# Gate logits in spare columns of the P·V bank, an earlier key load and one more GpSimd copy, in an attention + mixture-of-experts kernel

## The chip, the cores and the metric

The kernel runs on one core of one Trainium2 chip, as one launch. The metric is the device time of the launch in microseconds, median of the runs made: 671.96 us for the kernel before (three runs, 670.69 to 673.42 us).

## The reference

Attention over B = 4 batches, 8 heads, 768 positions of 64 features, then a mixture of 8 experts, two of them for each of the 3072 tokens:

```python
# attention, S=768, block=32, window=16, nb=24
k_sum = k.reshape(B, H, nb, block, D).max(axis=3)
v_sum = v.reshape(B, H, nb, block, D).mean(axis=3)
scores_l = where(|pos_i - pos_j| < 16, scale * q @ k.T, -1e9)
scores_s = scale * q @ k_sum.T + log(block)
a = softmax(concat([scores_l, scores_s], -1))
x = a @ concat([v, v_sum])                 # 3072 tokens x 512
# experts: w1 (8, 512, 1024), w2 (8, 1024, 512)
noisy = x @ w_gate + log1p(exp(x @ w_noise)) * noise
top2 = two largest of 8, weights = softmax of the two
out[token] = sum over its two experts e: weight * relu(x @ w1[e]) @ w2[e]
```

Each query sees its local window and one "block sum" for every block of 32 keys: the maximum of the block's keys (key maxima) and the mean of its values (block sums of V).

## The kernel before

**Stages.** Up to 138 us the attention and the gate run, then the expert products (lines 842 and 893) until 664 us, then the last stores. The attention is a loop `for t in range(-2, 23)` over 24 tiles of 128 tokens (6 tiles a batch), software-pipelined: an iteration t works on five tiles at once. In the order of issue an iteration does

- `load_q(t+5)` on SyncE's queue;
- `norm(t-1)`: VectorE reads the finished P·V tile `o` and writes `x` (lines 361, 365, 367);
- `scores(t+2)` on TensorE (316), `smax(t+2)` on VectorE (323, a row maximum `nm`), `p_trans(t+1)` on TensorE (339) into the two PSUM buffers named `pt`, which ScalarE copies out as `pts` (342); `mask_sums(t+3)` (306); `sexp(t+2)` on ScalarE (331); `kx_local(t+3)`, GpSimd copies of local keys;
- `av_space(t)`: the PSUM tile `o` (one buffer of two banks of 512 columns); `x_pe(t-1)` (376) into `pt` and ScalarE's copy `xt` of it; `av(t)` (352), the P·V product of tile t into `o`;
- `v_load(t+3)` and `x_out(t-2)` (the tile's `x` to DRAM as `xd`, line 371) on SyncE's queue.

Beside these stand the pieces of a table: `at(time, f, ...)` puts f into the iteration at a fractional time, and `run(t + 0.1)` and the like call what is due. An iteration issues the times t+0.02, t+0.1, t+0.3, t+0.31 and t+0.4 ahead of `av(t)`, and t+0.8 and t+0.9 behind it. The instructions of an engine run in the order of issue.

**The gate.** Tokens are gated in batches of four tiles. For batch b, with its four `xt` there, `gate_gt` (394) makes 32 logit rows of each tile on TensorE in a `pt` buffer, `gate_gc` copies them out as `lt` (VectorE, 402), `gate_gl` transposes that (408) into another `pt` buffer an iteration later, and `gate_gd` copies the result out as `lg` (415). For batches 0 to 3 these stand in iterations 5, 9, 13, 17 (`gate_gt`, `gate_gc`) and 6, 10, 14, 18 (`gate_gl`, `gate_gd`); for batch 4 both fall into iterations 21 and 22. Then `gate_a` (ScalarE), `gate_b` (VectorE, 439 to 451: the two largest of eight), `gate_m`, and `gate_c` (TensorE, 475 to 479) count and place the tokens; `gate_v` (528 to 578) builds lists.

**P·V's banks.** `o` is `[128, 2, 512]` in f32. `av` uses 4 x 65 = 260 columns of each bank (`GO` = 260). Behind them, the gate's small products (475 to 479) use columns 260 to 339 of the first bank.

**Keys and block sums.** Keys of batch b+1 come in two loads of three tiles, `load_k`, at the times `KL`; `k_piece` takes their block maxima on VectorE (230) at the times `KP`; `kx_sum` puts these into the score operand. `v_sums` makes the block sums of V on TensorE (256), copies them out, and makes some of the copies for the other tiles on GpSimd (272, 273); `v_rest` spreads the rest by DMAs from SBUF to SBUF (278, 281). All DMAs of the attention are issued by SyncE, in order, over eight semaphores: each waits for the landing of the one that is eight places earlier.

**Weights.** `w_load` brings weights (727, tile `stg`), ScalarE rounds them (`w_part`, 747 to 749), VectorE makes the remainders.

Of the kernel before, what the change touches and what calls it, by code (L numbers as in the profile page):

```python
# [8 lines left out]
F32 = mybir.dt.float32  # L9
# [11 lines left out]
P = 128  # L21
TS = S // P
NT = B * TS
# [40 lines left out]
def attn_moe(ctx, tc, qt, kt, vt, wgn, noise, w1, w2, out):  # L64
# [184 lines left out]
    def v_sums(b):  # L249
        if b:  # L250
            pt = psum.tile([P, HP, P], F32, name="pt", bufs=2).rearrange("p a b -> p (a b)")
        else:
            pt = psum.tile([P, 2, 512], F32, name="o")[:, 0]
        for j in range(TS):
            for g in range(4):
                nc.tensor.matmul(pt[32 * g:32 * g + NB, 0:C4], ind[:, j, :], VE[b % 2][:, j, C4 * g:C4 * g + C4],
                                 start=(j == 0), stop=(j == TS - 1), skip_group_check=True)
        x, y = VE[b % 2][W:W + NB], [z[0:NB] for z in VD[b % 2]]
        for g in range(4):
            i, o = pt[32 * g:32 * g + NB, 0:C4], slice(C4 * g, C4 * g + C4)  # L260
            if b == 3 and g % 2:
                nc.scalar.activation(x[:, 0, o], i, AF.Copy)
            elif b:
                nc.vector.tensor_copy(x[:, 0, o], i)
            else:
                nc.vector.tensor_copy(x[:, 0, o], i)
        if b == 1:
            nc.gpsimd.tensor_copy(y[0], x[:, 0])
        if b == 0:
            for i in range(3):  # L270
                if i:
                    nc.gpsimd.tensor_copy(x[:, i], x[:, 0])
                nc.gpsimd.tensor_copy(y[i], x[:, 0])

    def v_rest(b):
        x = VE[b % 2][W:W + NB]
        j = 1 if b else 3
        nc.sync.dma_start(x[:, j:], x[:, 0, None, :].to_broadcast([NB, TS - j, VB]))
        if b:
            for y in VD[b % 2][b == 1:]:  # L280
                nc.sync.dma_start(y[0:NB], x[:, 0])  # L281
# [104 lines left out]

    LT = {}

    def gate_gt(b):
        t0, t1 = BATCH[b]  # L390
        pt = psum.tile([P, HP, P], F32, name="pt", bufs=2)[:, 0]
        for c in range(DC):
            for i in range(GN):
                nc.tensor.matmul(pt[32 * i:32 * i + 32], wg32[:, c, :], XT[t0 + i][:, c, :],
                                 start=(c == 0), stop=(c == DC - 1), skip_group_check=True)
        LT[b] = pt
# [6 lines left out]
        else:  # L403
            nc.scalar.activation(LT[b], pt, AF.Copy)

    def gate_gl(b):
        pt = psum.tile([P, HP, P], F32, name="pt", bufs=2)[:, 0]
        nc.tensor.transpose(pt, LT[b], ident)
        LT[b] = pt

    def gate_gd(b):
        LG[b] = work.tile([P, GN, 16], F32, name="lg")
        x = LT[b].rearrange("p (t e) -> p t e", e=32)[:, :, 0:16]
        if b < 5:
            nc.vector.tensor_copy(LG[b], x)
        else:
            nc.scalar.activation(LG[b], x, AF.Copy)
# [507 lines left out]
    def at(t, f, *a):  # L925
        todo.setdefault(round(t, 3), []).append((f, a))
# [36 lines left out]
            at(W0[i] + 3 + k + 0.9, w_part, i, k, 0)  # L963
            at(W0[i] + 4 + k + 0.1, w_part, i, k, 1)
    VS = [5, 8, 15]
    KP = [-3, -3, -2, -1, 1, 2]
    KP0 = [1, 1, 1, 2, 2, 2]
    KL = [-6, -6, -6, -3, -3, -3]
    VL = [(0, 0, 0, 1, 1, 1), (4, 4, 5, 5, 6, 6), (10, 10, 11, 11, 12, 13)]
    for b in range(B - 1):  # L970
        for j in range(TS):
# [8 lines left out]
    for i in range(3):  # L980
        at(4.9 + 2 * i, fill, i)
    at(20.8, last_init)
    for t, i, k in ((19.9, 4, 0), (20.9, 4, 1), (21.9, 5, 0), (22.9, 5, 1), (22.9, 6, 0)):
        at(t, w_part, i, k, 0)
    for k in range(2):
        at(22.3, w_part, 4, k, 1)
# [4 lines left out]
    at(22.8, gate_p, 4)  # L991
    for b in (0, 1, 3, 2):
        u = BATCH[b][1] + 2
        at(u - 0.7, gate_gt, b)
        at(u - 0.6, gate_gc, b)
        at(u + 0.3, gate_gl, b)
        at(u + 0.4, gate_gd, b)
        at(u + 0.9, gate_a, b)
        at(u + 1.1, gate_b, b)
        at(u + 1.9, gate_m, b)  # L1000
        at(u + 2.9, gate_p, b)
        at(u + 2.3, lambda b, t: gate_c(b, PO[t]), b, u + 2)
        at(u + 3.02, lambda b, t: gate_d(b, PO[t]), b, u + 2)
        at(u + 3.9, gate_e, b)
        if b == 3:
            continue
        at(u + 4.1, gate_v, b)
        if b == 2:
            at(u + 4.2, gate_o0, b)
            at(u + 5.31, lambda b, t: gate_t0(b, PO[t]), b, u + 5)  # L1010
            at(u + 6.02, lambda t: gate_u0(PO[t]), u + 5)
            break
        z = u + 6
        at(z + 0.1, gate_o, b)
        at(z + 0.9, gate_f, b, (0,))
        at(z + 1.9, gate_f, b, (1,))
        at(z + 2.31, lambda b, t: gate_t(b, PO[t]), b, z + 2)
        at(z + 3.02, lambda b, t: gate_u(b, PO[t]), b, z + 2)
    at(20.1, decode, TB0[:, :, 0], TB0.bitcast(F32)[:, :, 1], 0, 3)
    at(21.3, gate_gt, 4)  # L1020
    at(21.4, gate_gc, 4)
    at(21.9, gate_gl, 4)
    at(22.02, gate_gd, 4)
    at(22.03, gate_a, 4)

    def run(t):
        for f, a in todo.pop(round(t, 3), []):
            f(*a)
# [5 lines left out]
    for t in range(-2, NT - 1):  # L1034
        if QBUF <= t + QA < NT:
            load_q(t + QA)
        u = t + 3
        if t >= 1:
            norm(t - 1, (lambda: kx_sum(u)) if u < NT else None)
        run(t + 0.02)  # L1040
        run(t + 0.03)
        if t + 2 < NT:
            scores(t + 2)
        if t == -1:
            q_piece(2)
            q_piece(3)
        run(t + 0.5)
        if t + 2 < NT:
            smax(t + 2)
        if 0 <= t + 1 < NT:  # L1050
            p_trans(t + 1, 0)
            p_trans(t + 1, 1)
        if t + 3 < NT:
            mask_sums(t + 3)
        if t + 2 < NT:
            sexp(t + 2, (0, 1) if t + 3 < NT else (0,))
        if u < NT and t >= 1:
            kx_local(u)
        run(t + 0.1)
        run(t + 0.2)  # L1060
        if t >= 0:
            av_space(t)
        run(t + 0.3)
        run(t + 0.31)
        if t >= 1:
            x_pe(t - 1)
        run(t + 0.4)
        if t >= 1:
            x_copy(t - 1)
        if t + 3 == NT:  # L1070
            sexp(t + 2, (1,))
        if t >= 0:
            av(t)
        run(t)
        run(t + 0.8)
        run(t + 0.9)
        if 0 <= t and t + 3 < NT:
            v_load(t + 3)
        if t >= 2:
            x_out(t - 2)  # L1080
# [7 lines left out]
    av(NT - 1)  # L1088
    gate_c(4, og)
    x_tr(0, 2, xp[:, 1].rearrange("p (a b) -> p a b", a=DC), False)  # L1090
    w_part(6, 1, 0)
    x_halves(0, 2, 0)
    x_pe(NT - 2)
    x_copy(NT - 2)
    norm(NT - 1)
    x_halves(0, 2, 1)
    w_part(7, 0, 0)
    w_part(7, 1, 0)
    gate_d(4, og)
    gate_e(4)  # L1100
    attn.close()
# [25 lines left out]
    for t in range(NT - 3, NT - 1):  # L1127
        x_out(t)
    low = {}
    for i in range(2):  # L1130
        bank()

    def first(f, mid=None):
        low[f] = mm1(0, 0, f, mid, False)
# [3 lines left out]
        x_copy(NT - 1)  # L1138

    def last_logits():  # L1140
        gate_gl(5)
        gate_gd(5)
        gate_a(5)

# [1 line left out]
    for x in HT:  # L1146
        nc.gpsimd.memset(x[:, :, CAPS[0]:], 0.0)
    x_out(NT - 1)
    gate_gt(5)
    gate_gc(5)  # L1150
    gate_v(3)
    low[0]()
# [3 lines left out]
    gate_p(5)  # L1156
    gate_o0(3)
    first(2)
    low[1]()
    gate_v(4)  # L1160
    first(3, lambda: gate_c(5, og))
# [198 lines left out]
```

## Time and profile before

| | before |
|---|---|
| median of three runs | 671.96 us (670.69 to 673.42) |
| profiled execution, its time | 675.12 us |
| its span, first to last instruction | 673.3 us |
| TensorE busy | 650.2 us (97%) |
| VectorE / ScalarE / GpSimd busy | 340.6 / 252.1 / 217.1 us |
| mean granted TensorE clock | 0.993 |

"Busy" is the time in which an engine has an instruction under way. Rows of the timeline begin with the start of a group of instructions and its duration, both in us; the brackets at the end of a row tell how long the engine idled before it and what it waited for. PE is TensorE, DVE VectorE, ACT ScalarE, POOL GpSimd, SP SyncE; `o<-hth,pts` reads "writes o, reads hth and pts". `hth`, `htl`, `ve`, `vd` are buffers that hold V in the attention. PEclk is the TensorE clock that the throttle granted, 1.00 being full speed.

### The profile page before, as it was taken

What the parts mean: (1) busy time and instruction counts of PE and PEld (TensorE: products, weight loads), DVE (VectorE), ACT (ScalarE), POOL (GpSimd) and SP (SyncE); (2) the same over time, 40 slices, a digit from 0 to 9 for tenths busy, and PEclk for the clock granted to TensorE, in tenths of its full rate; (3) what the DMA queues carried; (4) which work ended last, traced back from release to release, by engine and by line L of the source; (5) the groups of instructions that cost most, each with busy time, mean ns of one, the idle gap of its engine ahead of it and who ended that gap; (6) DMA issues with size and microseconds to landing.
All of it is one profiled execution on the core that took longest, in us unless ns stands there. A gap on an engine that the chain in (4) does not pass through costs nothing.

```text
span 673.3 us, 13939 instructions
## 1 busy us (share of the span) xinstructions
PE 650.2 (97%) x5485; PEld 379.9 (56%) x5485; DVE 340.6 (51%) x747; ACT 252.1 (37%) x570; POOL 217.1 (32%) x408
## 2 busy tenths in 40 slices
PE   8899799899999999999999999999999999999994
PEld 7678687655545544554455446544664455446541
DVE  5758799789794651265125513551264145312210
ACT  4867788841252450154015401530253045102100
POOL 4442134203265314431443144314431332321041
PEclk9999899999999999999999999999999999999998
DMA  9999999665297776267626753684378339521021
GB/s 299 309 276 297 307 311 320 226 219 140 108 258 210 213 177 211 85 172 174 211 84 173 186 190 96 177 203 152 95 197 229 121 86 234 148 76 48 1 92 48
DMA packets 93883, 120.50 MB, mean 179 GB/s; under 512 B 53577, under 2 KB 56913, under 8 KB 93808
## 3 DMA queue, kind: packets, MB, share of 16 engines
q1 hardware_dynamic: 82128, 83.24, 43.6%
q0 software_dynamic: 11680, 36.27, 16.9%
q8 instruction: 45, 0.74, 0.5%
q14 instruction: 30, 0.25, 0.1%
HBM read 82.03 MB, written 25.82 MB: 160 GB/s over the span
## 4 chain that ended last, share of the span: by engine, by line
PE 82%; DMA 9%; DVE 4%; SPq 2%; ACT 1%; issue 0%; POOL 0%; POOLq 0%; DVEq 0%; ACTq 0%
PE h L842 38%; PE pt L893 35%; DMA kb<-in_kt_dram 3%; PE h L893 2%; PE pt L890 2%; DMA xd<-x 2%; DMA htl<-in_vt_dram 2%; DMA ve<-ve 1%; PE pt L339 1%; DMA ve<-in_vt_dram 1%; DVE nm L323 1%; PE s L316 1%; PE o L352 1%; SPq L281 1%; DMA q<-in_qt_dram 1%; ACT p L331 1%
## 5 line engine op out<-in xcount | busy, mean ns | idle before, releaser
L842 PE MATMUL h<-xte,w1h 128*128 128x384 f16 (+4 forms) x1024 | 195.0, 331 | 1.1 <-DVE xte L818 1.1
L848 ACT ACTIVATE hth<-h 128x384 f16<-128x384 f32 (+4 forms) x128 | 63.7, 498 | 264.8 <-PE h L842 253.4
L842 PEld LDWEIGHTS <-w1h 128*128 128x128 f16 x1024 | 99.6, 98 | 73.0 <-issue 2.5
L89 POOL DMA_INDIRECT out_dram<-y,tb x48 | 52.9, 1101 | 234.4 <-DVE y L903 218.0
L893 PEld LDWEIGHTS <-hth 128*128 128x128 f16 x768 | 75.1, 98 | 89.3
L851 DVE SCALAR_TENSOR_TENSOR htl<-h,hth 128x384 f16<-128x384 f32 (+4 forms) x128 | 72.6, 568 | 70.0 <-ACT hth L848 63.7
L842 PE MATMUL h<-xte,w1l 128*128 128x384 f16 (+4 forms) x512 | 106.9, 331 | 0.0
L903 DVE SCALAR_TENSOR_TENSOR y<-pt,tb,prev 128x512 f32<-128x512 f32 x42 | 31.5, 751 | 144.9 <-PE pt L893 144.8
L89 POOL DMA_INDIRECT xg<-xd,tb x53 | 55.1, 1040 | 117.7 <-DVE x L806 68.9
L893 PE MATMUL pt<-w2l,hth 128*128 128x512 f16 x360 | 85.0, 379 | 0.0
L893 PE MATMUL pt<-w2h,hth 128*128 128x512 f16 x360 | 85.0, 379 | 0.0
L893 PE MATMUL pt<-w2h,htl 128*128 128x512 f16 x360 | 85.0, 379 | 0.0
L842 PEld LDWEIGHTS <-w1l 128*128 128x128 f16 x512 | 50.0, 98 | 35.5
L893 PEld LDWEIGHTS <-htl 128*128 128x128 f16 x384 | 37.6, 98 | 45.3
L754 DVE SCALAR_TENSOR_TENSOR w2l<-stg,w2h 128x1024 f16<-128x1024 f32 x28 | 34.3, 1225 | 38.4 <-ACT w2h L736 38.4
L331 ACT ACTIVATE p<-s,nm 128x120 f32<-128x120 f32 x192 | 51.1, 376 | 0.8
L736 ACT ACTIVATE w2h<-stg 128x1024 f16<-128x1024 f32 x28 | 29.5, 1054 | 54.2 <-DMA stg<-in_w_dram 54.2
L89 POOL DMA_INDIRECT prev<-out_dram,tb x42 | 43.8, 1043 | 13.2 <-issue 13.2
L754 DVE SCALAR_TENSOR_TENSOR w1l<-stg,w1h 128x1024 f16<-128x1024 f32 x28 | 34.3, 1224 | 21.1 <-ACT w1h L736 20.7
L736 ACT ACTIVATE w1h<-stg 128x1024 f16<-128x1024 f32 x28 | 29.4, 1050 | 11.4 <-DMA stg<-in_w_dram 11.4
L805 ACT ACTIVATE x<-xg 128x512 f16<-128x512 f32 (+4 forms) x48 | 29.8, 622 | 8.7 <-DVE y L901 3.7
L806 DVE TENSOR_TENSOR x<-xg,x 128x512 f16<-128x512 f32 (+4 forms) x48 | 32.7, 682 | 0.0
(225 smaller groups left out, 649.5 us busy)
## 6 DMA issues: line engine op xcount, KB each, us to landing
stg<-in_w_dram SPq DMA_DIRECT2D x64, 512.0 KB
q<-in_qt_dram SPq DMA_DIRECT2D x24, 256.0 KB
xd<-x SPq DMA_DIRECT2D x24, 256.0 KB
out_dram<-xg SPq DMA_DIRECT2D x8, 768.0 KB
kb<-in_kt_dram SPq DMA_DIRECT2D x6, 768.0 KB
hth<-in_vt_dram SPq DMA_DIRECT2D x12, 260.0 KB
htl<-in_vt_dram SPq DMA_DIRECT2D x16, 195.0 KB
ve<-in_vt_dram SPq DMA_DIRECT2D x12, 260.0 KB
```

What stands on the lines that cost most here:

```text
L89: return nc.gpsimd.indirect_dma_start(**kw)
L331: nc.scalar.activation(PE_[t][:, a, hp, :], SC[t][:, a, hp, :], AF.Exp, bias=NM[t][:, 1, a, hp:hp + 1], scale=0.125)
L736: nc.scalar.activation(WT[e][n + "h"][:, i % 4, :], SG[e, i], AF.Copy, scale=sc)
L754: nc.vector.scalar_tensor_tensor(lo, SG[e, i], sc, hi, op0=OP.mult, op1=OP.subtract)
L805: nc.scalar.activation(xs[:, :DM], x, AF.Copy)
L806: nc.vector.tensor_tensor(xs[:, DM:], x, xs[:, :DM], op=OP.subtract)
L842: nc.tensor.matmul(ph[:, :n], w[wn][:, c, f * P:(f + 1) * P], x[:, xo + c, c0:c1], start=(k == 0), stop=(k == 11))
L848: nc.scalar.activation(hh[:, f, c0:c1], ph[:, :n], AF.Relu)
L851: nc.vector.scalar_tensor_tensor(hl[:, f, c0:c1], ph[:, :n], 0.0, hh[:, f, c0:c1], op0=OP.max, op1=OP.subtract)
L890: nc.tensor.matmul(py[64 * i:64 * i + 64, :HD], hx[:, f, c * P:c * P + 64], wv[:, f, HD * i:HD * i + HD], start=st, stop=sp, skip_group_ch ...
L893: nc.tensor.matmul(py, hx[:, f, c * P:c * P + P], wv[:, f, :], start=st, stop=sp)
L903: nc.vector.scalar_tensor_tensor(y, py[:, :d], gw, pv[:, :d], op0=OP.mult, op1=OP.add)
```

## The change

Four things change.

1. `gate_gt` and `gate_gl` no longer take a `pt` buffer. They write 128 columns (340 to 467) of the first bank of the P·V tile that the iteration at hand uses: `PO[t]`, `PO[21]` for batch 4, and `og` for batch 5. For batch 4 the copy `lg` is made by ScalarE in place of VectorE.
2. The second key load of a batch is issued at -3.1 in place of -3, that is at the end of the iteration before, ahead of `v_load` and `x_out`.
3. The fourth key maximum of a batch is taken one iteration later (`KP`), those of the first prefetched batch one iteration later in four of six (`KP0`); `kx_sum(6)` is moved behind them.
4. `v_sums(0)` makes one more 24x520 copy on GpSimd, and the DMA of `v_rest(0)` carries two tiles in place of three. Some roundings of weights on ScalarE (`w_part`) stand later, and two empty takes of a PSUM bank ahead of the first expert are gone.

```diff
         if b == 0:
-            for i in range(3):
+            for i in range(4):
                 if i:
                     nc.gpsimd.tensor_copy(x[:, i], x[:, 0])
-                nc.gpsimd.tensor_copy(y[i], x[:, 0])
+                if i < 3:
+                    nc.gpsimd.tensor_copy(y[i], x[:, 0])
 
     def v_rest(b):
         x = VE[b % 2][W:W + NB]
-        j = 1 if b else 3
+        j = 1 if b else 4
...
-    def gate_gt(b):
+    GC = GO + 80
+
+    def gate_gt(b, o):
         t0, t1 = BATCH[b]
-        pt = psum.tile([P, HP, P], F32, name="pt", bufs=2)[:, 0]
+        pt = o[:, 0, GC:GC + P]
...
-    def gate_gl(b):
-        pt = psum.tile([P, HP, P], F32, name="pt", bufs=2)[:, 0]
+    def gate_gl(b, o):
+        pt = o[:, 0, GC:GC + P]
...
     def gate_gd(b):
-        if b < 5:
+        if b < 4:
             nc.vector.tensor_copy(LG[b], x)
...
-    KP = [-3, -3, -2, -1, 1, 2]
-    KP0 = [1, 1, 1, 2, 2, 2]
-    KL = [-6, -6, -6, -3, -3, -3]
+    KP = [-3, -3, -2, 0, 1, 2]
+    KP0 = [1, 1, 2, 2, 3, 3]
+    KL = [-6, -6, -6, -3.1, -3.1, -3.1]
...
-    for t, i, k in ((19.9, 4, 0), (20.9, 4, 1), (21.9, 5, 0), (22.9, 5, 1), (22.9, 6, 0)):
+    for t, i, k in ((19.9, 4, 0), (20.9, 4, 1), (22.9, 5, 0), (22.9, 5, 1)):
...
-        at(u - 0.7, gate_gt, b)
+        at(u - 0.69, lambda b, t: gate_gt(b, PO[t]), b, u - 1)
...
-        at(u + 0.3, gate_gl, b)
+        at(u + 0.3, lambda b, t: gate_gl(b, PO[t]), b, u)
...
-    at(21.3, gate_gt, 4)
+    at(21.31, lambda: gate_gt(4, PO[21]))
-    at(21.9, gate_gl, 4)
+    at(21.9, lambda: gate_gl(4, PO[21]))
...
-            norm(t - 1, (lambda: kx_sum(u)) if u < NT else None)
+            norm(t - 1, (lambda: kx_sum(u)) if u < NT and u != TS else None)
...
+        if u == TS:
+            kx_sum(u)
...
-    w_part(6, 1, 0)
+    w_part(6, 0, 0)
...
-    w_part(7, 0, 0)
-    w_part(7, 1, 0)
+    w_part(6, 1, 0)
...
-    for i in range(2):
-        bank()
...
-        gate_gl(5)
+        gate_gl(5, og)
...
-    gate_gt(5)
+    gate_gt(5, og)
...
+    for k in range(2):
+        w_part(7, k, 0)
```

What becomes of the order, at three places. Line numbers of the kernel after stand one to four higher.

TensorE in iteration 10, from the transpose of the gate's logits to the P·V product of tile 10. Before:

```order
L408 MATMUL pt<-ident,lt 128x128 [waits Activation_49]
L376 MATMUL pt<-ident,x 128x128 [waits DVE_49,Activation_49]
L376 MATMUL pt<-ident,x 128x128 x3
L352 MATMUL o<-ve,pts 64x65
L352 MATMUL o<-vd_100,pts 64x65 [waits DMAHW5_49]
```

After:

```order
L411 MATMUL o<-ident,lt 128x128 [waits DVE_49,PE_49]
L377 MATMUL pt<-ident,x 128x128 [waits Activation_49]
L377 MATMUL pt<-ident,x 128x128 x3
L353 MATMUL o<-ve,pts 64x65 [waits DVE_49]
L353 MATMUL o<-vd_100,pts 64x65 [waits DMAHW5_49]
```

The order is the same. The wait for VectorE's copy `lg` stood ahead of the transposes of `x` (376), which took the `pt` buffer after it; now the P·V product (353) has a wait for that copy, since both write or read the first bank of `o`. Iterations 6, 14 and 18 read alike; in 5, 9, 13, 17 and 21 the copy waited for is `lt`.

SyncE's queue, from the V load of tile 11 on (`htl<-in_vt_dram` is `v_load`, `hth<-hth` and `htl<-hth` are the block sums of batch 2, `kb_89` the second half of batch 3's keys). Before:

```order
L288 DMA htl<-in_vt_dram 96x520 [waits DMAHW1_49,PE_49]
L371 DMA xd<-x 128x512 [waits DMAHW2_49,DVE_49]
L111 DMA q_97<-in_qt_dram 128x512 [waits DMAHW3_49]
L278 DMA hth<-hth 24x5x520 [waits DMAHW4_49,DVE_49]
L281 DMA htl<-hth 24x520 [waits DMAHW5_49]
L281 DMA htl<-hth 24x520 [waits DMAHW6_49]
L281 DMA htl<-hth 24x520 [waits DMAHW7_49]
L106 DMA kb_89<-in_kt_dram 128x4x384 [waits DMAHW0_49,Pool_49]
```

After:

```order
L106 DMA kb_89<-in_kt_dram 128x4x384 [waits DMAHW1_49,Pool_49]
L289 DMA htl<-in_vt_dram 96x520 [waits DMAHW2_49,PE_49]
L372 DMA xd<-x 128x512 [waits DMAHW3_49,DVE_49]
L111 DMA q_97<-in_qt_dram 128x512 [waits DMAHW4_49]
L279 DMA hth<-hth 24x5x520 [waits DMAHW5_49,DVE_49]
L282 DMA htl<-hth 24x520 [waits DMAHW6_49]
L282 DMA htl<-hth 24x520 [waits DMAHW7_49]
L282 DMA htl<-hth 24x520 [waits DMAHW0_49]
```

The key load has moved up seven places, past the block sums' four transfers and three others, and these stand one place later.

VectorE in iterations 11 and 12: the row maximum of iteration 11, and what follows up to the key maximum of those keys. Before:

```order
L323 TENSOR_REDUCE nm<-s 128x8 [waits PE_49,Activation_49]
L230 TENSOR_REDUCE kmax<-kb_89 128x4x4 [waits DMAHW0_49]
L439 TENSOR_TENSOR nz<-sp,noi 128x32 [waits Activation_49]
L441 SCALAR_TENSOR_TENSOR nl<-lg,nz 128x32 [waits DVE_49]
L445 MAX mx<-nl 128x8 [waits DVE_49]
```

After, from the `norm` of iteration 12:

```order
L362 TENSOR_SCALAR r<-o 128x8 [waits PE_49]
L366 RECIPROCAL ri<-r 128x8 [waits DVE_49]
L368 TENSOR_TENSOR x<-o,ri 128x512 [waits DMAHW3_49,DVE_49]
L324 TENSOR_REDUCE nm<-s 128x8 [waits PE_49]
L750 SCALAR_TENSOR_TENSOR w1l_318<-stg,w1h_317 128x512 [waits DMAHW0_49,Activation_49]
L230 TENSOR_REDUCE kmax<-kb_89 128x4x4 [waits DMAHW1_49]
```

The first maximum of the second half of batch 3's keys, and with it VectorE's wait for their load, has moved from between the row maximum and `gate_b` of iteration 11 to behind the row maximum of iteration 12.

## The prediction

> **What bounds the kernel now.** I read the sums of three stretches first (busy time of each engine, granted clock, DMA share), then TensorE's waits in the first of them, then the timeline around each wait that the change touches.
>
> ```profile
> core 0: us, PE busy (x) PEld busy (x) DVE busy (x) ACT busy (x) POOL busy (x), PEclk, DMA share, GB/s
> 0.00:138.00 138.00, 123.85 (x2452) 99.77 (x2453) 106.38 (x338) 107.30 (x330) 45.47 (x108) 0.99 0.91 288
> 138.00:664.00 526.00, 526.00 (x3035) 280.16 (x3033) 233.45 (x410) 144.77 (x241) 170.62 (x299) 1.00 0.54 153
> ```
>
> From 138 to 664 us TensorE is busy in 526.00 of 526 us at full clock, and the change takes no matmul out of there. So the time can only move by what moves the start of the expert products at 138 us. Before it, TensorE idles 138.00 - 123.85 = 14.2 us. Its waits there that the change touches (us in total, times, longest):
>
> ```profile
> PE o L475 <- DVE x L367: 3.2, 1, 3.2
> PE pt L339 <- DVE lg L415: 1.4, 1, 1.4
> PE o L352 <- DMA hth<-hth: 1.2, 1, 1.2
> PE pt L339 <- ACT xt L382: 1.1, 3, 0.4
> PE pt L339 <- DVE r L361: 0.8, 1, 0.8
> ```
>
> The largest is at 79 us. The timeline of VectorE (start, duration, what it did, idle before it) shows where it comes from:
>
> ```profile
> 69.01 0.22 DVE L415 COPY lg<-pt 128x64 f32<-128x64 f32 x1
> ...
> 70.85 1.16 DVE L323 TENSOR_REDUCE nm<-s 128x8 f32<-128x960 f32 x1
> 75.60 0.69 DVE L230 TENSOR_REDUCE kmax<-kb 128x16 f32<-128x512 f32 x1 [3.59 <-DMA kb<-in_kt_dram]
> ...
> 78.17 0.16 DVE L361 TENSOR_SCALAR r<-o 128x8 f32<-128x8 f32 x1
> ...
> 78.60 0.69 DVE L367 TENSOR_TENSOR x<-o,ri 128x512 f32<-128x512 f32 x1
> ```
>
> The key maximum waits 3.59 us for the keys. Behind it, in VectorE's order, stand `gate_b` (until 78.17 us) and the norm of tile 11, whose `x` frees `o`. TensorE has run dry by then:
>
> ```profile
> 75.78 0.36 PE L306 MATMUL s<-mask,identb 64*64 64x384 bf16 x4
> 79.35 0.19 PE L475 MATMUL o<-m,tri 128*128 128x32 f16 x1 [3.21 <-DVE x L367]
> ...
> 79.49 0.94 PE L376 MATMUL pt<-ident,x 128*128 128x128 f32 x4
> 80.36 0.37 PE L352 MATMUL o<-hth,pts 120*64 120x65 f32 x1
> ...
> 82.29 1.41 PE L316 MATMUL s<-kx,q 64*64 64x120 f32 x32
> ...
> 91.25 0.27 PE L352 MATMUL o<-hth,pts 120*64 120x65 f32 x1
> ...
> 92.33 1.05 PE L316 MATMUL s<-kx,q 64*64 64x120 f32 x32
> ...
> 96.12 0.66 PE L376 MATMUL pt<-ident,x 128*128 128x128 f32 x4
> ```
>
> ```profile
> 76.00:79.60 3.60, 0.39 (x10) 0.26 (x7) 3.39 (x23) 0.63 (x2) 0.00 (x0) 1.00 1.03 354
> 79.60:83.20 3.60, 3.60 (x58) 3.15 (x60) 3.21 (x7) 2.78 (x11) 1.02 (x1) 0.53 1.07 334
> ```
>
> After that idle time the clock stands at 0.53 for the next 3.6 us. The transposes of x take 0.94 in place of 0.66 us, the P·V product 82.29 - 80.36 = 1.93 in place of 92.33 - 91.25 = 1.08, the scores 1.41 in place of 1.05: 0.28 + 0.85 + 0.36 = 1.5 us lost. [...]
>
> **The change part by part.** I keep two accounts: TensorE's, and VectorE's, because from 79 to 124 us VectorE works almost without a pause. In 79 to 126 us its norms waited for P·V this long:
>
> ```profile
> DVE r L361 <- PE o L352: 0.3, 1, 0.3
> ```
>
> So a pause of TensorE in that stretch is partly slack, and what reaches the end there is what VectorE loses or gains.
>
> *Key load and key maxima.* SyncE's issues around the load:
>
> ```profile
> 62.41 0.33 SPq L288 DMA_DIRECT2D htl<-in_vt_dram x1
> ...
> 68.48 0.61 SPq L106 DMA_DIRECT2D kb<-in_kt_dram x1
> 69.15 1.19 SPq L288 DMA_DIRECT2D htl<-in_vt_dram x1
> ```
>
> The load takes the place in the queue that had the issue at 62.41 us. Its issue at 68.48 ended the maximum's wait at 75.60, so about 7.1 us later; from 62.41 that gives 69.5 us, against a use that moves an iteration later, to about 77. I count the wait as gone: on VectorE +3.59 us, and +0.69 as the maximum itself leaves iteration 11, less 0.69 where it is added in iteration 12. On TensorE +3.21 and, if the idling before tile 12's product goes, the half clock's +1.5. For VectorE the half clock is worth less, at least the 0.3 us that its norm waited, at most the 1.5; I take 0.4, nearest to the row. What is late next: the seven issues passed, each one place later. The V load of tile 12 (issued 69.15, by the same 7.1 us there at 76.3) keeps its place; tile 12's product began at 80.36 and may come 3.2 us earlier, at 77.2. So 0.9 us of cover is left. The block sums of batch 2, of which one transfer now stands at 68.48, have the same end of use.
>
> *Gate in the bank of P·V.* The transposes of p no longer wait for `lg` or for the other takes of `pt`: TensorE +0.8 (its wait for `r`), +1.4 (for `lg`) and some of 1.1 us in three small waits; I take 0.4 of these, one of the three. In exchange P·V now waits for VectorE's copy. These are the starts of P·V and the copies:
>
> ```profile
> 68.56 0.27 PE L352 MATMUL o<-ve,pts 120*64 120x65 f32 x1
> ...
> 86.57 0.27 PE L352 MATMUL o<-hth,pts 120*64 120x65 f32 x1
> ...
> 111.18 0.27 PE L352 MATMUL o<-ve,pts 120*64 120x65 f32 x1
> ...
> 126.70 0.27 PE L352 MATMUL o<-ve,pts 120*64 120x65 f32 x1
> ```
>
> ```profile
> 86.72 0.28 DVE L402 COPY lt<-pt 128x128 f32<-128x128 f32 x1
> ...
> 92.52 0.21 DVE L415 COPY lg<-pt 128x64 f32<-128x64 f32 x1
> 92.65 0.15 DVE L361 TENSOR_SCALAR r<-o 128x8 f32<-128x8 f32 x1
> ...
> 113.74 0.22 DVE L415 COPY lg<-pt 128x64 f32<-128x64 f32 x1
> ...
> 127.37 0.29 DVE L402 COPY lt<-pt 128x128 f32<-128x128 f32 x1 [2.48 <-PE pt L376]
> ```
>
> End of copy less start of P·V: iteration 10, 69.23 - 68.56 = 0.67; 13, 87.00 - 86.57 = 0.43; 14, 92.73 - 91.25 = 1.48; 18, 113.96 - 111.18 = 2.78; 21, 127.66 - 126.70 = 0.96. In the other gate iterations the copy ends before P·V starts or within 0.2 us of it. Together 6.3 us on TensorE. Queued behind that product are the scores, the transposes and so the exponentials of the next tiles; and VectorE's next instruction, the norm's `r`, which waits for the product itself. At 92.65 `r` stood directly behind the copy; now P·V's 1.08 us and a hand-over stand between, some 1.2 us of VectorE in iteration 14 and again in 18. In iteration 10 the product is 0.67 later for VectorE too; in 13 the lists of the gate fill the wait (cost 0 for VectorE, at most 0.43). In 21 VectorE has pauses anyway (2.48 us before the copy), so there TensorE's numbers count: +1.4 + 0.4 - 0.96 = +0.8.
>
> [...] The order of the changed kernel has that wait, though P·V's columns are others than the copy's. Were waits set by columns, VectorE's sum below would be 1.2 + 1.2 + 0.7 us better.
>
> *One more copy on GpSimd, one tile less by DMA.*
>
> ```profile
> 20.37 0.62 POOL L273 COPY htl<-hth 24x520 f32<-24x520 f32 x1
> ...
> 29.57 0.35 POOL L129 COPY kx<-kmax 128x192 f32<-128x192 f32 x1 [6.66 <-DVE r L361]
> ```
>
> ```profile
> 32.42 0.33 PE L352 MATMUL o<-hth,pts 120*64 120x65 f32 x2 [1.18 <-DMA hth<-hth]
> 33.14 0.27 PE L352 MATMUL o<-htl,pts 120*64 120x65 f32 x1 [0.38 <-DMA htl<-in_vt_dram]
> ```
>
> GpSimd pays 0.62 us, and has 6.66 us without work soon after. Tile 3's product need not wait for that DMA (1.18 us), but the V load of the same tile ended 0.7 us later. The gain is between 0 and 1.2; I take 0.2, since the queue at a DMA share of 0.91 sets the next tile's load as before.
>
> *The rest.* `lg` of batch 4 by ScalarE, `w_part` later and the two empty takes of a bank: between 71 and 138 us these move under a microsecond of ScalarE from one place to another; I take 0, with 0.5 either way.
>
> **The sum.** VectorE's account to 124 us, then TensorE's: 0.2 - 0.67 + 3.59 + 0.69 - 0.69 + 0.4 - 1.2 - 1.2 + 0.8 = +1.9 us. TensorE's account alone: 0.2 + 3.2 + 1.5 + 0.8 + 1.4 + 0.4 - 6.3 = +1.2. I take +1.8, near VectorE's. The profiled execution took 675.12 us, 3.2 above the median of 671.96; against its own time the sum gives 673.3, against the median 670.2 us. What lies between the two is the same for both kernels, if the half clock occurs in the unprofiled runs too; were it absent there, 0.4 to 1.5 us of the gain go.
>
> **The rivals.** (A, the forecast) 670.2 us; between TensorE's account (670.8, and 671.5 with 0.5 from the rest and 0.2 from the early part against it) and VectorE's with the whole half clock, 1.1 more, and half of the early wait, 0.5 more: 668.6.
>
> (B) The new waits cost nothing: with the kmax wait gone VectorE is ahead of TensorE in iterations 10 to 18, the copies are done when P·V comes, and the pauses fall into slack. For it: VectorE lost its 3.6 us at one place and could keep the lead. Against it: in 14 and 18 it had no pauses before the copies, 20 and 35 us after. The sum without 0.67, 1.2 and 1.2 is 5.0: 667.0 us.
>
> (C) Slower: the pause before iteration 18's P·V, 2.78 us and longer if TensorE runs ahead, halves the clock as 3.21 us did before, for 1.5 us. Then TensorE's 1.2 becomes -0.3, and -0.8 with the 0.5 of ScalarE's moved work: 672.3 to 672.8 us. It decides from a pause of 3.2 us on at the latest, by the row at 79.35; no row here gives how much less is enough. [...]
>
> (D) The load's wait comes back as another: the DMA share is 1.03 to 1.07 from 76 to 83 us, and a load for tile 12 that lands 0.9 us late or more takes TensorE's gain there. With 0.9 of the 3.59 us kept, the sum is 1.9 - 2.7 = -0.8: 672.8 us.
>
> **How the numbers follow.** A 0.57, B 0.20, C 0.14, D 0.09. Half a per cent, 3.4 us, is about what a measurement of this kernel can tell from no change: faster is below 668.6, slower above 675.3. Faster has B and a small part of A, 0.05: 0.25. Slower has only what no case here reaches, a half clock and a late load together (672.8 + 2.7 = 675.5): 0.04. Same: 0.71. The range goes from 666.6, B with 0.4 to spare, to 673.1, D with 0.3 to spare.
>
> **What would show it.** Right: no wait of the key maximum near 72 us; P·V with waits for `lg` in iterations 10, 14 and 18, of 0.5 to 2.8 us; VectorE idle for over 1 us ahead of `r` in 14 and 18; the first expert product at about 136 us instead of 138. Wrong: P·V without such waits (B), a clock near 0.5 after 110 us (C), a wait of P·V or of scores for a load near 77 us (D), or expert products that begin elsewhere and still end at another distance.

## The result and the profile after

The kernel after takes 675.05 us (median of ten runs, 673.43 to 677.06), the kernel before 671.98 us (ten runs): a ratio of 1.005 (95% interval 1.0032 to 1.0068), by which it is 3.4 us slower (2.2 to 4.6; the medians lie 3.1 us apart). 670.2 us had been forecast, between 666.6 and 673.1. In a later measurement beside other kernels it was 677.89 against 671.05 us, 1.0106 (1.0075 to 1.0138). Why the two measurements differ by more than their intervals is not shown.

The profiled execution took 677.06 us, its span is 675.2 us. The same sums by stretch as before, the second now up to 666 us:

```profile
core 0: us, PE busy (x) PEld busy (x) DVE busy (x) ACT busy (x) POOL busy (x), PEclk, DMA share, GB/s
0.00:138.00 138.00, 122.82 (x2446) 99.55 (x2447) 104.76 (x330) 104.55 (x326) 45.96 (x109) 0.99 0.90 286
138.00:666.00 528.00, 526.87 (x3041) 280.74 (x3039) 235.19 (x416) 146.89 (x245) 170.47 (x299) 1.00 0.54 153
```

The expert products still take 526 to 527 us. Their first one starts at 139.80 us in place of 137.76, and the last ends 2.03 us later: the whole difference of the two profiled executions lies ahead of them. TensorE's waits in the first 140 us, the five largest of those that are new:

```profile
PE o L353 <- DVE lg L418: 5.3, 3, 2.6
PE s L317 <- issue: 1.9, 1, 1.9
...
PE pt L377 <- ACT pts L343: 1.5, 1, 1.5
...
PE pt L256 <- issue: 0.9, 1, 0.9
PE pt L340 <- issue: 0.8, 1, 0.8
```

The wait for `x` at 79 us is gone, and so are those of the transposes of p for `lg` and `r`. In their place P·V waits for `lg` three times, as the order had shown: in iterations 10, 14 and 18, on TensorE's timeline:

```profile
71.31 0.27 PE L353 MATMUL o<-ve,pts 120*64 120x65 f32 x1 [1.07 <-DVE lg L418]
...
91.16 0.27 PE L353 MATMUL o<-hth,pts 120*64 120x65 f32 x1 [1.59 <-DVE lg L418]
...
114.32 0.37 PE L353 MATMUL o<-ve,pts 120*64 120x65 f32 x1 [2.63 <-DVE lg L418]
```

And VectorE, which had taken `r` directly behind the copy, now stands idle between the two. Its timeline in 14 and 18:

```profile
90.89 0.21 DVE L418 COPY lg<-o 128x64 f32<-128x64 f32 x1
92.42 0.17 DVE L362 TENSOR_SCALAR r<-o 128x8 f32<-128x8 f32 x1 [1.31 <-PE o L353]
...
114.05 0.22 DVE L418 COPY lg<-o 128x64 f32<-128x64 f32 x1
116.43 0.17 DVE L362 TENSOR_SCALAR r<-o 128x8 f32<-128x8 f32 x1 [2.16 <-PE o L353]
```

Behind the third wait the granted clock falls to 0.55, as the windows of that place show. From its first matmul to that of the scores behind it P·V takes 2.01 us there (114.32 to 116.33) and 1.15 in iteration 14 (91.16 to 92.31), which is why VectorE's second pause is 2.16 us and the first 1.31:

```profile
110.00:114.00 4.00, 1.69 (x19) 1.21 (x17) 3.90 (x11) 3.46 (x13) 0.22 (x2) 1.00 1.04 373
114.00:117.60 3.60, 3.28 (x59) 3.16 (x63) 1.37 (x6) 1.03 (x4) 0.00 (x0) 0.55 0.72 263
```

"issue" in the list of waits means that no semaphore and no instruction of the program ended the wait; what ended a wait is called its releaser. Some 3.7 us of such waits had no place in the prediction; they are taken up below.

### The profile page after: what moved, and what is told of

It is laid out like the page before. It is cut to its first block, busy times and chain, and to the rows that moved or that the text cites. A ratio compares the mean times of both kernels' runs of the same rounds, so it can differ in the third digit from the quotient of the medians.

```text
span 675.2 us, 13946 instructions
## 1 busy us (share of the span) xinstructions
PE 650.1 (96%) x5485; PEld 380.3 (56%) x5485; DVE 340.7 (50%) x746; ACT 251.4 (37%) x571; POOL 217.4 (32%) x409
## 3 DMA queue, kind: packets, MB, share of 16 engines
q1 hardware_dynamic: 82104, 83.19, 43.4%
## 4 chain that ended last, share of the span: by engine, by line
PE 85%; DMA 9%; DVE 4%; ACT 1%; issue 1%; SPq 0%; POOL 0%; POOLq 0%; ACTq 0%
PE h L845 38%; PE pt L896 35%; DMA q<-in_qt_dram 4%; DMA htl<-in_vt_dram 2%; PE h L896 2%; PE pt L893 2%; PE o L353 2%; PE s L317 1%; PE pt L340 1%; DVE nm L324 1%; DMA kb<-in_kt_dram 1%; DMA stg<-in_w_dram 1%; DMA ve<-in_vt_dram 1%; PE o L397 1%; DVE x L368 1%; PE pt L377 1%
## 5 line engine op out<-in xcount | busy, mean ns | idle before, releaser
L343 ACT ACTIVATE pts<-pt 120x512 f32<-120x512 f32 x48 | 26.7, 610 | 20.3 <-PE pt L340 20.2
```

The costliest lines, as they stand in the source:

```text
L343: nc.scalar.activation(PT[t][:NK, a], pt[:NK], AF.Copy)
```

## The experiments

Ratios are to runs of the kernel before on the same chip. All kernels (two more, again and after_again, are single executions of 674.06 and 675.18 us, where the kernel before has medians of 672.06 and 671.47):

| kernel | time | ratio to before | 95% interval |
|---|---|---|---|
| after | 675.05 | 1.0050 | 1.0032 to 1.0068 |
| after, third measurement | 677.89 | 1.0106 | 1.0075 to 1.0138 |
| gate (gate's edit alone) | 678.47 | 1.0081 | 1.0051 to 1.0111 |
| keys (key load and maxima alone) | 672.20 | 1.0000 | 0.9981 to 1.0019 |
| vsum (GpSimd's copy alone) | 672.09 | 0.9993 | 0.9977 to 1.0009 |
| nogate (all but the gate's edit) | 671.53 | 0.9990 | 0.9970 to 1.0010 |
| old_keys (all but the key part) | 676.47 | 1.0073 | 1.0055 to 1.0091 |
| lt_only | 672.57 | 1.0002 | 0.9985 to 1.0020 |
| mid_out | 672.86 | 1.0018 | 1.0000 to 1.0035 |
| end_out | 677.06 | 1.0100 | 1.0071 to 1.0128 |
| early_lg | 674.63 | 1.0036 | 1.0020 to 1.0052 |
| gl4_out | 671.74 | 1.0013 | 0.9994 to 1.0033 |
| calm | 675.07 | 1.0062 | 1.0038 to 1.0085 |
| busy18 | 676.99 | 1.0083 | 1.0066 to 1.0101 |
| end_busy | 674.93 | 1.0058 | 1.0040 to 1.0077 |
| best | 671.11 | 0.9995 | 0.9979 to 1.0012 |

**The parts apart.** Three kernels make one part of the change on the kernel before, a fourth undoes one.

gate, the edits of `gate_gt`, `gate_gl`, `gate_gd` and their times alone:

> Before, with the gate's edit alone (logits and their transpose in P.V's bank, lg of batch 4 by ScalarE). Theory 1, the waits of P.V for the copies are what costs: P.V waits for lg in iterations 10, 14 and 18 (about 0.7, 1.5 and 2.7 us), the clock may fall once behind the last of them, no key load has moved, so nothing is gained: slower than before by 2 to 5 us, 674 to 677 us. Theory 2, what costs is the code of TensorE arriving late because the key load stands ahead of it in the DMA queues: this kernel leaves that order alone, so within 1.5 us of before.

keys:

```diff
-    KP = [-3, -3, -2, -1, 1, 2]
-    KP0 = [1, 1, 1, 2, 2, 2]
-    KL = [-6, -6, -6, -3, -3, -3]
+    KP = [-3, -3, -2, 0, 1, 2]
+    KP0 = [1, 1, 2, 2, 3, 3]
+    KL = [-6, -6, -6, -3.1, -3.1, -3.1]
```

(with `kx_sum(6)` moved; of the six entries of `KP0` three change, not four)

> Before, with the key load at -3.1 and the later key maxima alone. Theory 1: the 3.2 us wait at 79 us and the half clock behind it go, nothing is added: 3 to 5 us faster than before, 667 to 669 us. Theory 2: TensorE's code is late by about 2 us in iteration 10 (a wait that no instruction ends, near 66 us), so 0 to 2.5 us faster.

vsum, four copies by GpSimd in place of three, and the smaller transfer:

> Before, with the fourth copy by GpSimd alone and the smaller transfer. Theory 1: 0.2 us faster. Theory 3, the smaller transfer shifts the landings of the first 40 us so that scores of the second tile wait for q (0.7 us) or code comes late (0.8 us at 41 us): 0.5 to 1.5 us slower at the start of iteration 0, and as much at the end if nothing later takes it up.

nogate, the kernel after with the first of its four parts undone:

> The kernel after, with the gate's edit undone (logits again in a buffer of their own), so that keys, GpSimd's copy and the moved weight roundings remain. Theory 1: 3 to 5 us faster than before. Theory 2: the stop in iteration 10 near 66 us is there as in the kernel after (about 2 us), so 0 to 2.5 us faster than before.

The gate's edit alone costs 0.81%, 5.4 us: theory 1. Its profile has the same three waits for `lg`, 5.2 us together. The other parts together gain nothing that can be measured: 0.10%, 0.7 us, with an interval on both sides of none. So the loss is the gate's edit, and the expected gain of the key part isn't there. Why not, the next run tells.

**Was the wait for the keys a property of the kernel?** again is the kernel before without any edit.

> The kernel before, unchanged, profiled once more. Theory A, the 3.2 us wait at 79 us (key maximum on its load) and the half clock behind it belong to every execution of this kernel: both are there again, the first expert product at about 137.8 us. Theory B, they belonged to the one profiled execution, which took 3.2 us more than the median: the key maximum waits 2 us or less, TensorE under 1 us there, the clock stays at 1.00 from 70 to 90 us, and the first expert product starts near 135 us.

In this second execution VectorE's timeline at the place where the maximum had waited 3.59 us reads

```profile
72.74 1.16 DVE L323 TENSOR_REDUCE nm<-s 128x8 f32<-128x960 f32 x1
73.82 0.68 DVE L230 TENSOR_REDUCE kmax<-kb 128x16 f32<-128x512 f32 x1
```

with no wait, and the windows show a full clock:

```profile
76.00:79.60 3.60, 3.60 (x76) 2.86 (x72) 3.48 (x8) 3.21 (x10) 0.00 (x0) 1.00 1.07 373
79.60:83.20 3.60, 3.28 (x72) 2.61 (x67) 3.01 (x8) 3.33 (x12) 2.81 (x4) 1.00 1.03 364
```

Theory B. The three other kernels with the old place of the key load, gate, vsum and old_keys, have the maximum wait 0, 0.86 and 0 us there. One of five executions had the long wait, and it was the one that the prediction was worked out from. The first expert product started at 136.74, not near 135: this execution, of 674.06 us, had 4.1 us of stops with "issue" as the releaser, and a half clock at 130 us.

**How the gate's 5 us divide.** In early_lg the pieces that stood ahead of `lg` on VectorE are issued behind P·V:

```diff
-        at(u + 4.1, gate_v, b)
+        at(u + 4.8, gate_v, b)
-            at(u + 4.2, gate_o0, b)
+            at(u + 4.9, gate_o0, b)
```

> The kernel after, with the list pieces of the gate (gate_v, gate_o0) issued behind P.V of their iteration in place of ahead of it, so that on VectorE the copy lg no longer stands behind them. If P.V's waits for lg are what costs (theory 1): these waits fall from 1.1, 1.6 and 2.6 us to under 0.7 each, the clock does not fall after 112 us, and the time falls by 4 to 6 us to 669 to 671 us, at or below before. If something else of the edit costs (late code, the rest of the moved work): 673 us or more.

lt_only puts the transposed logits back:

```diff
     def gate_gl(b, o):
-        pt = o[:, 0, GC:GC + P]
+        pt = psum.tile([P, HP, P], F32, name="pt", bufs=2)[:, 0]
```

> The kernel after, with the transposed logits (gate_gl) back in a buffer of their own and only the logits themselves (gate_gt) in P.V's bank. Theory 1, the waits for lg are the cost and those for lt are not: 671 to 672.5 us, as with the whole edit undone. If the waits for lt cost as much, 673 to 674.

old_keys has the three tables of the key part as before:

> The kernel after, with the key load and the key maxima as before. The gate's edit alone took 678.5 us, the whole change 675.05. If the key part is what makes the difference (it shortens what stands ahead of lg on VectorE, or takes waits away): about 678. If the moved weight roundings and GpSimd's copy make it: 675 to 676.

lt_only came out as expected, to 0.1 us: with `gate_gl` alone out of P·V's bank, the loss is gone (1.0002). The logits themselves may stay there. old_keys lies between its two branches. early_lg did to the waits and the clock what was expected and not to the time. TensorE's waits for `lg` fell from 5.3 to 0.4 us, but in its profile other waits stand in their place:

```profile
PE pt L340 <- issue: 2.2, 2, 1.5
PE s L317 <- issue: 1.8, 2, 1.1
PE pt L377 <- ACT pts L343: 1.7, 1, 1.7
PE pt L256 <- issue: 1.4, 1, 1.4
PE o L353 <- DVE lt L405: 1.4, 1, 1.4
...
PE o L353 <- DVE lg L418: 0.4, 1, 0.4
```

The third of these is at the end of the attention. ScalarE's timeline there, early_lg first:

```profile
129.68 0.22 ACT L420 ACTIVATE lg<-o 128x64 f32<-128x64 f32 x1 [1.36 <-DVE x L368]
...
130.34 1.07 ACT L343 ACTIVATE pts<-pt 120x512 f32<-120x512 f32 x2
```

and lt_only, where `lg` is read from another buffer:

```profile
127.27 0.22 ACT L420 ACTIVATE lg<-pt 128x64 f32<-128x64 f32 x1
...
127.92 1.07 ACT L343 ACTIVATE pts<-pt 120x512 f32<-120x512 f32 x2
```

The copy of batch 4 is ScalarE's now, and reads the tile that the norm reads on VectorE: it waits 1.36 us for it (0.58 us in the kernel after), and `pts` behind it on ScalarE, and TensorE for `pts`. So two more kernels undo that alone, on early_lg and on the kernel after, and a third undoes the middle alone.

gl4_out, early_lg with `gate_gl` in `o` only for `b < 4`:

> early_lg, with the transposed logits of batch 4 alone back in a buffer of their own. Theory: at the end of the attention the copy lg of batch 4 waits for the norm that reads the same bank, and ScalarE's pts stands behind it (1.7 us at 130 us against 0.35 us in lt_only). Then 1 to 1.7 us faster than early_lg, 673 to 673.6 us. If the end hides it: as early_lg, 674.6.

end_out, the kernel after with the same edit:

> The kernel after, with the transposed logits of batches 4 and 5 alone back in a buffer of their own; batches 0 to 3 stay in P.V's bank. If the end of the attention costs 1.3 us (pts behind lg behind the norm), and the waits for lg in iterations 10, 14 and 18 with the half clock the rest of the 3.2 us that lt_only gained: 673.5 us, 0.3% above before. If the waits in the middle are nearly all: 674.5 to 675. If the end is nearly all: 672.

mid_out, the kernel after with `gate_gl` in `o` only for `b > 3`:

> The kernel after, with the transposed logits of batches 0 to 3 back in a buffer of their own; batches 4 and 5 stay in P.V's bank. No wait of P.V for lg in 10, 14 and 18 and no half clock, but the 1.5 us wait of the transposes of x for pts near 131 us stays: by the same split 673.5 us; if the waits in the middle are nearly all, 672; if the end is nearly all, 674.5 to 675.

gl4_out fell further than expected (to 1.0013, from early_lg's 1.0036), and lt_only's 1.0002 lies below mid_out's 1.0018; the intervals of either pair overlap. So the end is worth 1 to 1.5 us by these pairs, not clear of the noise. The middle, the waits in iterations 10, 14 and 18, is the rest: mid_out is at most 0.35% above before, the kernel after 0.5 to 1.1%. end_out missed by 3 us on the slow side. When the kernel after was measured once more, below, it too took 677.89 us (1.0106), so end_out is not shown to be slower than its base; and with the middle's waits left the end gains nothing that shows.

The starts of P·V in the traces divide the loss by place (first row: executions without a stop with "issue" as the releaser there; second row: such stops, up to 1.5 us, taken off):

| stretch | with the waits for `lg` | without |
|---|---|---|
| P·V of tile 9 to tile 11 | 9.3 us (after_again, after_third) | 8.5 to 8.8 (before, again, nogate, vsum, best) |
| P·V of tile 11 to tile 19 | 43.4 to 43.8 (three executions of the kernel after); 42.3 and 42.7 (end_busy, old_keys, both at full clock) | 39.0 to 39.4 (keys, nogate, lt_only, mid_out, best) |
| P·V of tile 19 to the first expert product | 19.5 to 19.7 (three executions of the kernel after) | 21.6 (before, keys, nogate, vsum) |

So the middle costs 0.5 to 0.8 and 4.0 to 4.8 us, and 1.8 to 2.1 us come back behind it: 2.4 to 3.8 us in all, where the first measurement has 3.4. At full clock, about 3.1 us in end_busy and 3.4 in old_keys, of the 3.3 and 4.2 us that P·V waited there in iterations 14 and 18, are found again at tile 19.

**The clock behind the third wait.** after_third is the kernel after unchanged; the two others have useless matmuls ahead of P·V of iteration 18, written to spare columns of the scores' buffer of tile 21 (`SR`), where they disturb the sums of that tile's scores, so that these two kernels compute something else and only their times are of use; everything else is as it was:

```diff
+        SR[t] = gate_space()
...
+    def keep_busy(t, n):
+        for i in range(n):
+            nc.tensor.matmul(SR[t][:, 0, SK:512], identb, identb[:, 0:512 - SK], start=True, stop=True,
+                             skip_group_check=True)
+
+    at(18.4, keep_busy, 21, 36)
```

> The kernel after, unchanged, on the chip of the two runs beside it, as their base: 675 us, 0.5% above before, with P.V's waits for lg of 1.1, 1.6 and 2.6 us and the clock near 0.8 from 110 to 120 us.

> The kernel after, with 36 small matmuls without use (32 columns each, into columns of the scores' buffer that nobody reads) ahead of P.V of iteration 18, where TensorE waits 2.6 us for lg. P.V starts no earlier. If the half clock behind that wait comes from the pause and costs 1.5 us: the clock stays at 1.00 from 110 to 120 us and the time is 1 to 1.5 us below after_third. If the half clock costs nothing in the end, VectorE setting the pace: equal within 0.5 us. If the pause isn't its cause: the clock falls as before.

> end_out (677.06 us, 3.3 us more than expected, with granted clocks down to 0.988) with the same 36 matmuls ahead of P.V of iteration 18. If its extra time comes from half clocks behind that pause: 673 to 674.5 us and clocks of 0.995 or more. If it comes from late code (stops of 1.7 us at 66 and 1.5 us at 96 us in its profile): 676 us or more.

The small matmuls went by in 0.9 us and left a pause of 1.7 us in place of 2.6. In end_busy that was enough, in busy18 not; the windows of 115 to 120 us of end_out, end_busy and busy18:

```profile
115.00:120.00 5.00, 5.00 (x85) 4.38 (x85) 2.70 (x6) 1.56 (x5) 0.00 (x0) 0.70 0.89 320
```

```profile
115.00:120.00 5.00, 5.00 (x121) 4.19 (x121) 4.19 (x21) 2.88 (x11) 0.00 (x0) 1.00 0.90 323
```

```profile
115.00:120.00 5.00, 3.60 (x64) 3.27 (x64) 2.60 (x10) 2.10 (x7) 0.00 (x0) 0.66 0.94 341
```

From P·V of tile 18 to that of tile 19 took 5.55 us in end_out (114.99 to 120.54) and 4.22 in end_busy (114.41 to 118.63): 1.3 us for the half clock, where 1.5 had been worked out. end_busy is 0.4% below end_out, with intervals that just overlap, its expectation missed by 0.4 us; busy18 against after_third (1.0083, 1.0106) doesn't tell.

One pause of 1.7 us was followed by the half clock, the other not. What goes with this difference was counted over all traces. The record of the clock gives 3.413 us for the half clock at 79.67 us in before and for that at 114.35 in the kernel after. In each trace the starts of the half clocks, the one after 660 us included, lie whole multiples of 3.413 us apart: 79.667 and 666.759 us in before (172.0 times), 114.351 and 670.723 in the kernel after (163.0 times). Cut into windows at these multiples (a trace with only one such start is cut from that), with edges that lie otherwise in each execution, the time from 10 to 140 us of the 19 traces has 690 windows at full clock. In nine of them TensorE was busy for less than 0.47 of the window, and all nine were followed by a half clock; of ten with 0.48 to 0.54 four were, of the other 671 none. The window ahead of the drop is at 0.09 in before and 0.23 in the kernel after. The pause of busy18 lay within one window (busy 0.49), that of end_busy was cut by an edge at 112.90 us (busy 0.56 behind it), and that of 2.65 us in old_keys by one at 109.69 (0.57 and 0.56). What in the chip makes it so no run here shows. The window of the pause in the kernel after, and the two in old_keys:

```profile
110.94:114.35 3.41, 0.78 (x10) 0.54 (x7) 3.23 (x11) 3.00 (x11) 0.00 (x0) 1.00 1.04 383
```

```profile
106.27:109.69 3.42, 1.94 (x21) 1.30 (x18) 3.32 (x8) 2.49 (x9) 0.71 (x3) 1.00 1.05 380
109.69:113.10 3.41, 1.90 (x60) 1.83 (x64) 1.99 (x9) 2.22 (x8) 0.00 (x0) 1.00 1.03 399
```

**Late code.** after_again is the kernel after, unchanged:

> The kernel after, unchanged, profiled once more. What belongs to the kernel comes again: P.V's waits for lg in iterations 10, 14 and 18 (1.1, 1.6, 2.6 us within 0.2) and the 1.5 us wait of the transposes of x for pts near 131 us. What belonged to one execution may not: the stops for late code (0.8 us at 41, 1.9 us at 66, 0.9 us at 96 us). If all these stops come again within 0.5 us, they belong to the order of this kernel.

The waits for `lg` (1.15, 1.45, 2.63) and for `pts` (1.50) came again, so they belong to the kernel. Of the stops without a releaser those at 41 and 96 us came again (1.63 and 1.48 us), the one of 1.95 us at 66 us did not. This is what it looks like on TensorE, in the middle of the scores of one tile:

```profile
65.30 0.37 PE L317 MATMUL s<-kx,q 64*64 64x120 f32 x4
67.61 0.63 PE L317 MATMUL s<-kx,q 64*64 64x120 f32 x12 [1.95 <-issue]
```

In the order of TensorE's recorded instructions, semaphore waits counted with the matmuls and weight loads, the kernel after's three stops have 1474, 2498 and 3521 instructions ahead of them: 1024 apart, give or take one. And all 64 stops of over 0.2 us with this releaser in the traces of all kernels, up to 140 us, have 193 plus a multiple of 256 ahead of them, or one more. The page has a DMA queue that it calls instruction,

```profile
q8 instruction: 45, 0.74, 0.5%
```

with 45 packets of 16 KB; in the first 140 us of the kernel after it moved 19 of them, for 4986 of these instructions, and each such stop ends 1.2 to 1.8 us after one of these packets. In the kernel after the packets ahead of the three stops began 3.7, 5.0 and 6.8 us after the start of the instruction 256 places ahead of the stop, at a DMA share of 1.06, 1.06 and 0.94 in between; the longest such delay is 7.4 us (in busy18, at 0.92). That these packets hold TensorE's code, that the stops wait for it (late code) and that it stood behind data is inferred from this. calm tried to thin those out:

```diff
-        at(W0[i], w_load, 0, i)
+        at(W0[i] + 1, w_load, 0, i)
```

> The kernel after, with each of the first four weight loads (512 KB) issued one iteration later. Theory of late code: one of them stands ahead of the code fetch of iteration 10, whose delay of 5.0 us falls to about 3, and the stop of 1.9 us near 66 us is under 0.5: 1 to 2 us faster than the kernel after, 673 to 674 us. If those stops cost nothing in the end, or come from the key load alone: 675.

The packet of iteration 10 came with a delay of 0.7 us in place of 5.0, the stop at 66 us was gone, and the time was the same (675.07). In that execution another packet, its delay counted from 86 us on, came after 6.3 us, with a stop of 0.7. So a single such stop doesn't decide the time. Theory 2, that late code behind the moved key load is the loss, is refuted by gate, old_keys (no moved load, 0.7 to 0.8% slower) and keys (moved load, equal). Nor do such stops by themselves make the loss, wherever they come from: the profiles of lt_only, mid_out and gl4_out have 4.1 to 4.8 us of them in the first 140 us, those of the kernel after 3.7 to 4.5, and these three kernels are at most 0.2% above before.

**A version without the loss.** best keeps the logits out of P·V's bank and takes what the other parts offer: the key part, GpSimd's copy, the roundings, the list pieces behind P·V, and `lg` of batch 4 by ScalarE, of which this edit against the kernel before is the last:

```diff
     def gate_gd(b):
-        if b < 5:
+        if b < 4:
```

> No gate logits in P.V's bank: the kernel before with the key and GpSimd parts, the moved weight roundings, lg of batch 4 by ScalarE and the list pieces behind P.V. TensorE's waits for the buffer that lg holds (0.8 us at 109 us, 1.4 us at 125 us) should be short: 1 to 2 us faster than nogate (671.5), 669.5 to 670.5 us, 0.3% below before. If those waits were hidden: 671 to 672.

Its profile has neither the wait of 0.8 nor that of 1.4 us, its profiled execution took 668.94 us, but the median of twelve runs is 671.11 against 671.47: no difference. No kernel here is measurably faster than the kernel before.

## Why the prediction was wrong

**What bounds the kernel: right.** Only the start of the expert products moved, by 2.04 us, and the end by 2.03 with it.

**The key wait, the step that failed first.** "I count the wait as gone: on VectorE +3.59 us", with 0.4 to 1.5 for the half clock: the wait did go, but there was none to remove in most executions. The row was right and its execution was not the usual one: 675.12 us against a median of 671.96, and the text took the 3.2 us between the two as the same for both kernels. Shown by again (no wait, full clock) and keys (1.0000). Measured size of the term: 0, with 1.3 us either way by the interval of keys. Without its 4.0 us the forecast's +1.8 becomes -2.2, or 674.2 us, which is within the first measurement's interval (674.1 to 676.6); the step below is what gate shows beyond it.

**P·V's waits: the sizes were right, the account was not.** 0.67, 1.48 and 2.78 us were forecast, 1.07, 1.59 and 2.63 came. VectorE's pauses ahead of `r`, forecast as 1.2 each, were 1.31 and 2.16. The step that failed is "so a pause of TensorE in that stretch is partly slack": for the gate's edit alone VectorE's account gave -0.67 - 1.2 - 1.2 + 0.8 = -2.3 us, TensorE's +0.8 + 1.4 + 0.4 - 6.3 = -3.7 us, and with the half clock -5.2; gate measured -5.4 (-3.4 to -7.5). Up to P·V of tile 19 most of it came through, as the table of the stretches shows; what came back is behind that tile, about 2 us where the account had 0.8 (1.8 without its wait for `lt`, which was absent). That VectorE, set back by the same waits, had no lead to give is the likely reason and is not shown. The first measurement alone would not refute VectorE's account, gate does.

**Rival C was the right mechanism.** Behind the pause in iteration 18 the clock did fall to half: the pause was 2.63 us long in after, after_again, after_third and end_out, 2.64 in gate and 1.83 in calm, though the clock stayed at full in old_keys behind 2.65 us, where the pause fell into two windows. It was given 0.14, and a time that still had the 3.2 us of the key wait and the 1.5 of its half clock in it; without these its -0.3 to -0.8 becomes -5.0 to -5.5, and the two measurements of the kernel after are 3.1 and 6.8 us above before. Its condition, a pause of 3.2 us "at the latest", was the only one the row before could give, and shorter pauses came with the drop too, 2.63 us in the kernel after and 1.35 in keys: in the window ahead of the drop TensorE was busy for 0.23 of the time in the kernel after, and for up to 0.54 in others (keys).

**The copy's columns.** P·V did wait for the copy of other columns of its bank, 5.3 us in three waits. These waits come from the order that was built; whether the chip would have needed them no run here shows.

**"The rest: I take 0", wrong by 1 to 1.5 us, as far as the two pairs show it.** ScalarE's copy of batch 4 has a new wait, 0.58 us in the kernel after and 1.36 in early_lg, with `pts` behind it, for which TensorE waits 1.5 and 1.7 us. The prediction counted the copy's work and not whom it must wait for on a shared tile.

**Smaller points.** GpSimd's copy: +0.2 forecast, within its interval (0.9993). The wait for `lt` in iteration 21, forecast as 0.96, was absent in the kernel after and 1.4 us in early_lg, lt_only and old_keys. B and D did not come. Stops for late code were in no term; they differ between executions of one kernel (0 and 4.1 us in before and again), and the part of the loss that they make in the median stays open, as does why stops of 0.4 us and more between 55 and 100 us came in 12 of the 13 profiles with the gate's edit or a part of it, and in one of the six without (again; before, keys, vsum, nogate and best had 0.3 us at most).

## What to carry to other kernels

A wait read from one profiled execution is worth a term only if that execution is near the median, or if a second one shows it; 3.2 us above the median is about the size of the wait that was going to be saved. Before a result is put into spare columns of a tile that another engine's work passes through, list everyone who writes or reads that tile in the same iteration: here P·V came to wait for the copy `lg`, 5.3 us in three waits, and of two readers on two engines one waited for the other, ScalarE's `lg` of batch 4 for VectorE's norm (0.58 us in the kernel after, 1.36 in early_lg). When two accounts of the same edit differ (the busy engine's and its partner's slack), the slack must be shown to survive the edit's own waits.

## What the runs showed of the hardware

- TensorE's granted clock fell to half for 3.41 us (before, the kernel after), or twice that in gate (0.67 from 110 to 120 us), behind pauses of 1.35 us (keys) to 3.21 us (before), a stop of 2.49 us with "issue" as the releaser among them (gl4_out, mid_out), and stayed at full behind others as long (2.65 us in old_keys, 1.75 in end_busy). So the length of the pause alone did not tell the two apart here. How little TensorE worked in one window, cut at multiples of 3.413 us from the trace's own half clock, went with it: 0.09 and 0.23 busy ahead of the drop in before and the kernel after, 0.49 in busy18, against 0.57 and 0.56 without one in old_keys and 0.56 in end_busy; over all 19 traces nine windows under 0.47 were all followed by the half clock, 671 over 0.54 never, and ten in between either way.
- In the kernel after TensorE stood still three times with "issue" as the releaser, for 0.8, 1.9 and 0.9 us, with 1474, 2498 and 3521 recorded instructions ahead (1024 apart, give or take one), and each stop ended 1.2 to 1.5 us behind a 16 KB packet of the queue that the page calls instruction. The packets had come 3.7, 5.0 and 6.8 us after the instruction 256 places ahead of the stop, at a DMA share of 0.94 to 1.06. In the kernel before, the first execution has no stop over 0.2 us, again has 4.1 us of them; the most is 5.6 us in one execution (end_out).
